# A fused attention read and ReLU-squared FFN on one core: the opening parts go from six to four, and GpSimd's steps of the weights and of batches 0 and 1 go to VectorE

## The chip, the core and the metric

The kernel runs on one core of a Trainium2 chip. The metric is the device time of one execution in microseconds (us), as the median of several runs. A core has TensorE (PE, with weight loads PEld), VectorE (DVE), ScalarE (ACT), GpSimd (POOL) and SyncE (SP), which here only issues DMAs. Each engine takes its instructions in order from a queue of its own.

## What is computed

Inputs are x (8 batches, 8 heads, 512 rows, 64 columns), a state (8, 8, 32, 64), and the weights w_in (512 x 2048) and w_out (2048 x 512), which come as float64.

```python
scores = scale * x @ state.T            # per batch and head: 512 x 32
a = softmax(scores);  xread = a @ state            # 512 x 64
a2 = softmax(scale * state @ x.T);  sread = a2 @ x # 32 x 64
x = concatenate([xread, sread])         # per batch 544 rows x 512
h = x @ w_in;  r = maximum(h, 0);  out = (r * r) @ w_out
```

## The kernel before, in words

**Precision.** Each product of float32 values is made of three matmuls of rounded parts: `split` (L96) writes hi, the rounded copy (ScalarE, L97), and lo, the rest (a subtraction, L98, on the engine that its last argument names). So a, z, g and the weights all have a hi and a lo tile.

**Weights.** w_in and w_out come as pairs of 32-bit words. `singles` (L100) makes float32 of 128 x 512 of them with one ScalarE instruction (L107) and four on VectorE: L108, L109 (one input each), L113, L117 (two inputs). There are 16 pieces of w_in (tiles w_raw, wf) and 16 of w_out (wo_raw, wof), that is 32 conversions. They share four buffers (tag "raw", RAW = 4), which L113 and L117 read last. The wo pieces are then split (L453), with wo_lo on GpSimd.

**z in place of w_in.** Since xread = a @ state, the kernel multiplies the state by w_in first (z_part, tile pz, L192 for the first six pieces and L204 later), stores z in device memory (zd) and reads it back for each batch and pair of column tiles (z_fetch, L230). Batches 0 to 3 use the first set of z, batches 4 to 7 a second set, which is made during batches 2 and 3.

**Attention.** For each batch two groups of four heads: scores (L291 or L301), a transposition (L306), the softmax over the state (soft1 and soft1b: maximum L317, subtraction L318, exponential L319 on ScalarE, sum L324, reciprocal L326, product L327), a transposition back (at, L329), and the split into a_hi and a_lo. L318 and L327 (tile q) are on GpSimd for batches 0 to 2 and on VectorE from batch 3; a_lo is on GpSimd for all.

**The FFN** (mlp, L383 on) goes in units: one column tile of 128 of w_in's 2048 columns (fc, 0 to 15) for one batch's 512 rows. `up` makes ph from a and z with six matmuls (L394), then r = relu (L396), the square (ScalarE L398 for the first ten units, VectorE L400 after that) and g_hi, g_lo. `down` makes twelve matmuls into four accumulators po (L420), two units behind.

**Order of the work.** Every batch needs all 16 pieces of both weights, which have to be loaded and converted first. So batches 0 and 1 are taken in parts, listed in BOTH: entry (b, c) means that batch b goes on up to column tile c. At the end of a part its four accumulators are copied to the tile `sum` (L439, L441) or added to it (L601). Steps of the weights and of the attention are spread over the units by due times (class Ahead): a weight's steps are due shortly before the first unit that needs its tile, the attention of a batch before that batch's first unit (2 x begins[b] - 1). From what is written out so, a scheduler sets the order on each engine, moving instructions ahead by its own estimate. SyncE's queue holds all loads and the stores of wf (wd, L165) and reads of zd (L230) in one order: a store that waits for VectorE, or a read that waits for an earlier store of zd, holds back the loads behind it.

Of the kernel before, what the change touches and what calls it, by code (L numbers as in the profile page):

```python
# [18 lines left out]
def memory_attention_then_relu2_ffn(  # L19
# [22 lines left out]
    nc = tc.nc  # L42
    P = 128
# [3 lines left out]
    N = stT.shape[1] // (H * B)  # L47
# [5 lines left out]
    NFC = DF // P  # L53
# [10 lines left out]
    XRAW = 2  # L64
    PLAIN_Z = 6
    PLAIN_X = 2
    BOTH = ((0, 2), (1, 6), (0, 10), (1, 10), (0, NFC), (1, NFC))
    LATE = 3

    def pool_early(early):  # L70
        return nc.gpsimd if early else nc.vector
# [11 lines left out]
    wo = [None] * NFCH  # L83
# [12 lines left out]
    def split(hi, lo, src, eng_lo):  # L96
        nc.scalar.copy(out=hi, in_=src)  # L97
        eng_lo.tensor_sub(out=lo, in0=src, in1=hi.bitcast(F32))  # L98

    def singles(out_f, words):  # L100

        low, high = words[..., 0], words[..., 1]
        bits = out_f.bitcast(I32)
        nc.scalar.activation(out_f, high.bitcast(F32), AF.Abs)  # L107
        nc.vector.tensor_scalar_max(out_f, out_f, 2.0**-15)  # L108
        nc.vector.tensor_scalar(  # L109
            out=bits, in0=bits, scalar1=3, scalar2=0x3FFFFFF8,  # L110
            op0=ALU.logical_shift_left, op1=ALU.bitwise_and,
        )
        nc.vector.scalar_tensor_tensor(  # L113
            out=bits, in0=high, scalar=-0x40000000, in1=bits,
            op0=ALU.bitwise_and, op1=ALU.bitwise_or,
        )
        nc.vector.scalar_tensor_tensor(  # L117
            out=bits, in0=low, scalar=29, in1=bits,
            op0=ALU.logical_shift_right, op1=ALU.bitwise_or,
        )  # L120
# [138 lines left out]
    def attention_group(b, g, pair):  # L259
        CG = C // NG  # L260
        NQ = CG // P
        NJ = S // 32
# [51 lines left out]
        def soft1():  # L314
            q1 = my["q1"]
            m1 = sb.tile([P, NJ, 1], F32, name="m1", bufs=2)
            nc.vector.tensor_reduce(out=m1[:, :, 0], in_=q1, axis=AX.X, op=ALU.max)  # L317
            pool_early(b < 3).tensor_sub(out=q1, in0=q1, in1=m1.broadcast_to([P, NJ, N]))  # L318
            nc.scalar.activation(q1, q1, AF.Exp)  # L319

        def soft1b():
            q1 = my["q1"]
            s1 = sb.tile([P, NJ, 1], F32, name="s1", bufs=2)
            nc.vector.tensor_reduce(out=s1[:, :, 0], in_=q1, axis=AX.X, op=ALU.add)  # L324
            nc.vector.tensor_scalar_add(s1, s1, EPS)
            nc.vector.reciprocal(s1, s1)  # L326
            pool_early(b < 3).tensor_mul(out=q1, in0=q1, in1=s1.broadcast_to([P, NJ, N]))  # L327
            at = sb.tile([P, S], F32, name="at", bufs=2)
            nc.vector.transpose(out=at, in_=q1.rearrange("p j n -> p (j n)"))  # L329
            split(pair[0][:, g, :], pair[1][:, g, :], at, nc.gpsimd)  # L330

        def cut_n():
            hl = sb.tile([P, NT, NQ, 2, P], F32R, name="xn_hl", tag="x_hl", bufs=1)
# [19 lines left out]
        def read():  # L353
# [16 lines left out]
            for q in range(NQ):  # L370
                for i in range(2):
# [5 lines left out]
                    )  # L377

        names = (load_t, cut_t, scores, soft1, soft1b, load_n, cut_n, turn, read)
        return {f.__name__: f for f in names}  # L380

# [61 lines left out]
    def wo_load(fc):  # L443
        k, i = divmod(fc, FPC)
        raw = sb.tile([P, DM, 2], I32, name="wo_raw", tag="raw", bufs=RAW)
        nc.sync.dma_start(
            out=raw.rearrange("p e w -> p (e w)"), in_=w_out[fc * P:(fc + 1) * P, :]
        )
        wf = sb.tile([P, DM], F32, name="wof", bufs=2)
        singles(wf, raw)  # L450
        if i == 0:
            wo[k] = [const.tile([P, FPC, DM], F32R, name=f"{n}{k}") for n in ("wo_hi", "wo_lo")]
        split(wo[k][0][:, i, :], wo[k][1][:, i, :], wf, nc.gpsimd)  # L453


    parts, upto = [], [0] * B
    for b, c in BOTH + tuple((b, NFC) for b in range(2, B)):
        parts.append((b, range(upto[b], c)))
        upto[b] = c

    begins, ends, at = {}, {}, {}
# [79 lines left out]
    for m in range(NFC):  # L541
        steps = []
        if m + 2 < NFC:
            steps.append(z0[m + 2][1])
        if m + 4 < NFC:
            steps.append(z0[m + 4][0])
        steps.append(lambda m=m: wo_load(m))
        if m >= 2:
            steps += z0[m][3]
        if m + 2 < NFC:  # L550
            steps.append(z0[m + 2][2])
        weights.add(steps, 2 * min(at[m], at[m - m % FPC] - 2))
# [62 lines left out]
    for i in range(NGB):  # L615
        pt = ps_x.tile([P, NCC, P], F32, name="pt2", tag="px")
        for cc in range(NCC):
            nc.tensor.transpose(
                out=pt[:, cc, :], in_=sr[i][:, cc * P:(cc + 1) * P], identity=ident
# [56 lines left out]
```

## Time and profile before

| | |
|---|---|
| median of 3 runs | 734.75 us (734.13 to 735.08) |
| profiled execution | 734.07 us, its span 732.2 us |
| TensorE busy | 679.1 us, 93% of the span |
| VectorE busy | 476.6 us, 65% |
| ScalarE busy | 392.7 us, 54% |
| GpSimd busy | 197.6 us, 27% |
| DMA | 90.52 MB, 124 GB/s over the span |
| granted TensorE clock, mean | 0.963 |

The page cuts the span into 40 slices of 18.3 us and gives each engine's busy share in tenths. In a row of a group stand: line, engine, operation, output<-input, shape, count | busy us, mean ns | idle us just before, and what ended it. In a row of the timeline stand: start and length in us, engine, line, operation, and in brackets the idle time before it with its releaser. Shares over the whole span hide that the opening and the rest have different limits, so the stages are read apart.

### The profile page before, as it was taken

The numbers are of one execution on the slowest core, as the hardware profiler recorded it, in microseconds if no ns is written. First come the engines' busy times: TensorE is split into PE (matmuls) and PEld (weight loads), VectorE is DVE, ScalarE is ACT, GpSimd is POOL, SyncE is SP. The second block draws the span as 40 slices with busy tenths as digits, with TensorE's granted clock in tenths as the row PEclk, the third lists the DMA queues.
The fourth block names the chain that finished last, engine by engine and source line by source line (L and its number), as shares of the span: only waits on it lengthen the run. The fifth ranks groups of instructions, "written<-read, shape, count | busy, mean of one in ns | idle before, by whom it ended". The sixth has DMA issues, their size and how long they took to land.

```text
span 732.2 us, 9312 instructions
## 1 busy us (share of the span) xinstructions
PE 679.1 (93%) x3152; PEld 554.3 (76%) x3152; DVE 476.6 (65%) x797; ACT 392.7 (54%) x711; POOL 197.6 (27%) x181
## 2 busy tenths in 40 slices
PE   4865898889999899999999999999999999999994
PEld 1434677768888788888888878878888888888893
DVE  5889798798956944356954694797755445443541
ACT  2656477566766664357654554656554345332441
POOL 2334121146662540025402322343152022000000
PEclk9677799999999999999999999999999999999998
DMA  9757877684464641143433211422141012100410
GB/s 265 252 175 249 243 244 235 201 221 133 133 213 129 195 127 59 47 140 119 136 108 116 86 59 58 143 87 86 60 144 58 31 33 82 42 1 9 135 59 30
DMA packets 72435, 90.52 MB, mean 124 GB/s; under 512 B 3780, under 2 KB 55748, under 8 KB 72388
## 3 DMA queue, kind: packets, MB, share of 16 engines
q1 hardware_dynamic: 54980, 73.15, 32.2%
q10 hardware_dynamic: 17408, 16.78, 6.8%
q8 instruction: 25, 0.41, 0.3%
q14 instruction: 22, 0.18, 0.1%
HBM read 60.03 MB, written 29.88 MB: 123 GB/s over the span
## 4 chain that ended last, share of the span: by engine, by line
PE 74%; DMA 11%; DVE 8%; ACT 3%; issue 2%; SPq 0%; POOL 0%; ACTq 0%; DVEq 0%
PE po L420 43%; PE ph L394 23%; DMA wo_raw<-w_out 3%; DMA z_raw<-zd 3%; PE pr L357 2%; PE pz L204 2%; DMA xn_raw<-xn 2%; DMA st_f<-stT 1%; PE pq L291 1%; DMA zd<-z_stage 1%; DVE sp_hl L252 1%; PE pz L192 1%; DVE wof L113 1%; DVE wof L117 1%; PE pt L345 1%
## 5 line engine op out<-in xcount | busy, mean ns | idle before, releaser
L420 PE MATMUL po<-wo_hi,g_hi 128*128 128x512 f32 x544 | 219.1, 405 | 15.5 <-ACT g_hi L97 12.1
L420 PE MATMUL po<-wo_lo,g_hi 128*128 128x512 f32 x544 | 216.4, 399 | 0.0
L400 DVE TENSOR_TENSOR ph<-ph,r 128x512 f32<-128x512 f32 (+1 forms) x134 | 89.0, 664 | 152.0 <-ACT r L396 151.9
L396 ACT ACTIVATE r<-ph 128x512 f32<-128x512 f32 (+1 forms) x144 | 82.6, 574 | 168.1 <-PE ph L394 167.4
L420 PE MATMUL po<-wo_hi,g_lo 128*128 128x512 f32 x544 | 152.4, 392 | 0.4
L420 PEld LDWEIGHTS po<-wo_hi,g_hi 128*128 128x128 f32 x544 | 103.9, 191 | 39.9 <-ACT g_hi L97 14.7
L420 PEld LDWEIGHTS po<-wo_lo,g_hi 128*128 128x128 f32 x544 | 104.9, 193 | 20.3 <-issue 0.7
L420 PEld LDWEIGHTS po<-wo_hi,g_lo 128*128 128x128 f32 x544 | 101.3, 189 | 22.0 <-DVE g_lo L98 1.6
L98 DVE TENSOR_TENSOR g_lo<-ph,g_hi 128x512 fp32r<-128x512 f32 (+1 forms) x144 | 94.5, 656 | 34.2 <-ACT g_hi L97 24.6
L97 ACT CAST g_hi<-ph 128x512 fp32r<-128x512 f32 (+1 forms) x144 | 81.1, 563 | 43.0 <-DVE ph L400 37.8
L394 PE MATMUL ph<-a_hi,z_hi 128*128 128x512 f32 x256 | 81.4, 399 | 0.6 <-DVE g_lo L98 0.6
L394 PE MATMUL ph<-a_hi,z_lo 128*128 128x512 f32 x256 | 79.7, 393 | 0.0
L394 PE MATMUL ph<-a_lo,z_hi 128*128 128x512 f32 x256 | 79.3, 391 | 0.0
L98 POOL TENSOR_TENSOR xn_hl<-xn_raw,xn_hl 128x1024 fp32r<-128x1024 f32 x16 | 39.2, 2449 | 147.9 <-ACT xn_hl L97 79.6
L183 POOL TENSOR_TENSOR w<-wf,w 64x512 fp32r<-64x512 f32 x32 | 43.5, 1360 | 59.6 <-ACT w L182 52.5
L394 PEld LDWEIGHTS ph<-a_hi,z_lo 128*128 128x128 f32 x256 | 48.4, 189 | 11.0 <-DVE z_lo L98 0.3
L394 PEld LDWEIGHTS ph<-a_hi,z_hi 128*128 128x128 f32 x256 | 47.8, 193 | 11.5 <-DVE g_lo L98 1.3
L394 PEld LDWEIGHTS ph<-a_lo,z_hi 128*128 128x128 f32 x256 | 48.2, 189 | 10.3
L98 DVE TENSOR_TENSOR z_lo<-z_raw,z_hi 128x512 fp32r<-128x512 f32 x64 | 50.2, 784 | 4.3 <-ACT z_hi L97 4.3
L97 ACT CAST z_hi<-z_raw 128x512 fp32r<-128x512 f32 x64 | 39.4, 615 | 12.3 <-DMA z_raw<-zd 11.9
L98 POOL TENSOR_TENSOR xt_hl<-xt_raw,xt_hl 128x1024 fp32r<-128x1024 f32 x12 | 29.3, 2438 | 58.5 <-ACT xt_hl L97 36.0
L98 POOL TENSOR_TENSOR wo_lo<-wof,wo_hi 128x512 fp32r<-128x512 f32 x16 | 22.5, 1407 | 79.4 <-ACT wo_hi L97 79.4
(98 smaller groups left out, 854.4 us busy)
## 6 DMA issues: line engine op xcount, KB each, us to landing
zd<-z_stage ACTq DMA_DIRECT2D x64, 256.0 KB
z_raw<-zd SPq DMA_DIRECT2D x63, 256.0 KB
xt_raw<-xT SPq DMA_DIRECT2D x16, 512.0 KB
w_raw<-w_in SPq DMA_DIRECT2D x16, 512.0 KB
wo_raw<-w_out SPq DMA_DIRECT2D x16, 512.0 KB
xn_raw<-xn SPq DMA_DIRECT2D x16, 512.0 KB
out<-sum SPq DMA_DIRECT2D x32, 256.0 KB
wd<-wf SPq DMA_DIRECT2D x16, 256.0 KB
```

Source lines behind the costliest of these rows:

```text
L97: nc.scalar.copy(out=hi, in_=src)
L98: eng_lo.tensor_sub(out=lo, in0=src, in1=hi.bitcast(F32))
L113: nc.vector.scalar_tensor_tensor(out=bits, in0=high, scalar=-0x40000000, in1=bits, op0=ALU.bitwise_and, op1=ALU.bitwise_or,)
L117: nc.vector.scalar_tensor_tensor(out=bits, in0=low, scalar=29, in1=bits, op0=ALU.logical_shift_right, op1=ALU.bitwise_or,)
L183: nc.gpsimd.tensor_sub(out=w[other], in0=wf[own], in1=w[own].bitcast(F32))
L192: nc.tensor.matmul(pz[:, q, :], lhsT=st["raw"][own, h, :], rhs=box["wf"][own, q, :], start=True, stop=True,)
L204: nc.tensor.matmul(pz[:, q, :], lhsT=a[:, h, :], rhs=w, start=j == 0, stop=j == len(todo) - 1,)
L357: nc.tensor.matmul(pr[:, q].rearrange("p i c -> p (i c)"), lhsT=my["e"][:, t, q].rearrange("p i n -> p (i n)"), rhs=my["xn"][:, t, q].rear ...
L394: nc.tensor.matmul(ph, lhsT=w, rhs=v, start=i == 0, stop=i == len(todo) - 1)
L396: nc.scalar.activation(r, ph, AF.Relu)
L400: nc.vector.tensor_mul(out=ph, in0=ph, in1=r)
L420: nc.tensor.matmul(po[t], lhsT=g, rhs=w, start=i == 0 and j == 0, stop=i == last and j == 2)
```

## The change

Batches 0 and 1 are taken in four parts instead of six: batch 0's tiles 0 to 5, batch 1's 0 to 9, batch 0's 6 to 15, batch 1's 10 to 15. Before: batch 0's 0 and 1, batch 1's 0 to 5, batch 0's 2 to 9, batch 1's 6 to 9, batch 0's 10 to 15, batch 1's 10 to 15. And three kinds of steps go from GpSimd to VectorE: L318 and L327 for batches 0 and 1 (8 instructions), a_lo for batches 0 and 1 (4), and wo_lo (16).

```diff
-    BOTH = ((0, 2), (1, 6), (0, 10), (1, 10), (0, NFC), (1, NFC))
+    BOTH = ((0, 6), (1, 10), (0, NFC), (1, NFC))
...
-            pool_early(b < 3).tensor_sub(out=q1, in0=q1, in1=m1.broadcast_to([P, NJ, N]))
+            pool_early(b == 2).tensor_sub(out=q1, in0=q1, in1=m1.broadcast_to([P, NJ, N]))
...
-            pool_early(b < 3).tensor_mul(out=q1, in0=q1, in1=s1.broadcast_to([P, NJ, N]))
+            pool_early(b == 2).tensor_mul(out=q1, in0=q1, in1=s1.broadcast_to([P, NJ, N]))
...
-            split(pair[0][:, g, :], pair[1][:, g, :], at, nc.gpsimd)
+            split(pair[0][:, g, :], pair[1][:, g, :], at, pool_early(b >= 2))
...
-        split(wo[k][0][:, i, :], wo[k][1][:, i, :], wf, nc.gpsimd)
+        split(wo[k][0][:, i, :], wo[k][1][:, i, :], wf, nc.vector)
```

Order on TensorE after the first two units, before; ph_456 and ph_513 are the up products of units 2 and 3, a_hi_289 is batch 1's attention:

```order
L394 MATMUL ph_456<-a_hi_289,z_hi_459 128x512
L394 MATMUL ph_456<-a_hi_289,z_lo_460 128x512 x2
L394 MATMUL ph_456<-a_lo_290,z_hi_459 128x512
L394 MATMUL ph_513<-a_hi_289,z_hi_459 128x512
L394 MATMUL ph_513<-a_hi_289,z_lo_460 128x512 x2
L394 MATMUL ph_513<-a_lo_290,z_hi_459 128x512
```

The same units on TensorE in the changed kernel; a_hi_109 is batch 0's attention, z_hi_401 its z of tiles 2 and 3, and pz_534 is z of tile 6:

```order
L394 MATMUL ph_398<-a_hi_109,z_hi_401 128x512 x2
L394 MATMUL ph_508<-a_hi_109,z_hi_401 128x512 x2
L204 MATMUL pz_534<-w2_0_430,stz_lo_125 128x256
L204 MATMUL pz_534<-w2_0_430,stz_hi_124 128x256
L394 MATMUL ph_398<-a_hi_109,z_lo_402 128x512 x2
L394 MATMUL ph_398<-a_lo_110,z_hi_401 128x512 x2
L394 MATMUL ph_508<-a_hi_109,z_lo_402 128x512 x2
L394 MATMUL ph_508<-a_lo_110,z_hi_401 128x512 x2
```

Units 2 and 3 are now batch 0's tiles 2 and 3, with new z, instead of batch 1's tiles 0 and 1.

Order on VectorE just ahead of the seventh g_lo (unit 6, g_lo_695), before; wof_609 and wof_700 are pieces 6 and 7 of w_out, counted from 0:

```order
L113 SCALAR_TENSOR_TENSOR wof_609<-wo_raw_607,wof_609 128x512
L117 SCALAR_TENSOR_TENSOR wf_758<-w_raw_589,wf_758 128x512
L117 SCALAR_TENSOR_TENSOR wof_609<-wo_raw_607,wof_609 128x512
L108 TENSOR_SCALAR wof_700<-wof_700 128x512
L109 TENSOR_SCALAR wof_700<-wof_700 128x512
L98 TENSOR_TENSOR w2_1_741<-wf_669,w2_0_740 128x512
L113 SCALAR_TENSOR_TENSOR wof_700<-wo_raw_698,wof_700 128x512
L98 TENSOR_TENSOR g_lo_695<-ph_678,g_hi_694 128x512
```

On VectorE in the changed kernel, a little ahead of the seventh g_lo; a_lo_311 is batch 1's attention, wo_lo2_393 and wo_lo3_531 belong to pieces 5 and 6 of w_out, po0_479 is batch 0's first accumulator:

```order
L98 TENSOR_TENSOR wo_lo2_393<-wof_445,wo_hi2_392 128x512
L329 STREAM_TRANSPOSE at_687<-q1_573 128x512
L109 TENSOR_SCALAR wf_811<-wf_811 128x512
L117 SCALAR_TENSOR_TENSOR wof_524<-wo_raw_522,wof_524 128x512
L98 TENSOR_TENSOR w2_1_794<-wf_703,w2_0_793 128x512
L108 TENSOR_SCALAR wof_632<-wof_632 128x512
L441 COPY sum_736<-po0_479 128x512
L113 SCALAR_TENSOR_TENSOR wf_811<-w_raw_607,wf_811 128x512
L98 TENSOR_TENSOR a_lo_311<-at_687,a_hi_310 128x512
L441 COPY sum_736<-po2_481 128x512
L98 TENSOR_TENSOR wo_lo3_531<-wof_524,wo_hi3_530 128x512
```

The moved steps stand between the conversions now, and the last a_lo of batch 1, which unit 6 needs, comes after the conversion of piece 6 of w_out. On GpSimd the first steps after its memsets are those of batch 2 (xt_hl).

## The prediction

> **What bounds the kernel now.** I read the page's slices first, then the busy times by stage, then what TensorE waits for, then VectorE's instruction groups up to 160 us, then single instructions.
>
> ```profile
> PE   4865898889999899999999999999999999999994
> DVE  5889798798956944356954694797755445443541
> PEclk9677799999999999999999999999999999999998
> ```
>
> TensorE is busy nine tenths and more from the ninth slice on. Only the first nine of forty (18.3 us each, to 165 us) and the last have room, and there VectorE is at 7 to 9 tenths.
>
> ```profile
> core 0: us, PE busy (x) PEld busy (x) DVE busy (x) ACT busy (x) POOL busy (x), PEclk, DMA share, GB/s
> 0.00:100.00 100.00, 68.87 (x222) 45.51 (x223) 79.12 (x142) 54.16 (x103) 30.55 (x32) 0.80 0.76 235
> 100.00:163.00 63.00, 55.14 (x264) 44.58 (x262) 54.73 (x86) 39.69 (x75) 15.54 (x12) 0.97 0.74 226
> 163.00:240.00 77.00, 76.82 (x360) 63.98 (x361) 58.72 (x102) 53.51 (x95) 41.51 (x34) 0.98 0.49 151
> 240.00:732.00 492.00, 478.24 (x2310) 400.26 (x2308) 284.05 (x471) 245.34 (x442) 110.01 (x106) 0.99 0.26 84
> ```
>
> TensorE idles 31.1 us before 100 us, 7.9 us from 100 to 163, 0.2 us from there to 240, and 13.8 us later, which the change does not touch. What the opening saves by the moment TensorE stops waiting (163.2 us) is saved at the end. What that moment waits for:
>
> ```profile
> 160.19 1.65 DVE L117 SCALAR_TENSOR_TENSOR wof<-wo_raw,wof 128x512 int32<-128x512 int32 x1
> ...
> 164.16 0.68 DVE L98 TENSOR_TENSOR g_lo<-ph,g_hi 128x512 fp32r<-128x512 f32 x1
> ```
> ```profile
> 99.51 0.40 PE L420 MATMUL po<-wo_hi,g_hi 128*128 128x512 f32 x1
> ...
> 163.18 0.77 PE L420 MATMUL po<-wo_hi,g_hi 128*128 128x512 f32 x1 [2.58 <-ACT g_hi L97]
> ```
>
> TensorE's last wait there (2.58 us, at 163.18) ends when ScalarE rounds the 17th unit's g, and in front of its square on VectorE (in-order) stands the last weight conversion; 164.16 is the 17th g_lo. I use "17th g_lo" as the mark. A unit is one column tile of one batch; 163.18 is the down product of number 16, counted from 0, and 99.51 that of number 6. So VectorE's queue up to that mark sets the opening, with the loads that it waits for.
>
> **The change, part by part.** First the price of a moved step. VectorE alone, and beside GpSimd:
>
> ```profile
> 72.44 0.68 DVE L113 SCALAR_TENSOR_TENSOR wof<-wo_raw,wof 128x512 int32<-128x512 int32 x1
> 73.05 0.68 DVE L117 SCALAR_TENSOR_TENSOR wf<-w_raw,wf 128x512 int32<-128x512 int32 x1
> ...
> 75.19 0.41 DVE L109 TENSOR_SCALAR wf<-wf 128x512 int32<-128x512 int32 x1
> ```
> ```profile
> 53.35 1.49 POOL L98 TENSOR_TENSOR a_lo<-at,a_hi 128x512 fp32r<-128x512 f32 x1 [4.36 <-ACT a_hi L97]
> 53.64 1.24 DVE L325 TENSOR_SCALAR s<-s 128x16 f32<-128x16 f32 x1
> 56.05 1.10 POOL L327 TENSOR_TENSOR q<-q,s 128x512 f32<-128x512 f32 x1 [1.21 <-DVE s L326]
> 56.17 1.53 DVE L113 SCALAR_TENSOR_TENSOR wf<-w_raw,wf 128x512 int32<-128x512 int32 x1
> ```
>
> Alone, a 128x512 step with two inputs lasts 0.68 us and the next starts 0.60 after it; one with one input lasts 0.41. Beside a GpSimd step the same L113 lasts 1.53, and a 16-column step 1.24. What this costs VectorE in the first 160 us (the last column is its idle time):
>
> ```profile
> L113 DVE SCALAR_TENSOR_TENSOR wf<-w_raw,wf 128x512 int32<-128x512 int32 x16 | 15.2, 949 | 0.1
> L113 DVE SCALAR_TENSOR_TENSOR wof<-wo_raw,wof 128x512 int32<-128x512 int32 x16 | 13.3, 834 | 0.1
> L117 DVE SCALAR_TENSOR_TENSOR wof<-wo_raw,wof 128x512 int32<-128x512 int32 x15 | 12.5, 831 | 0.1
> L117 DVE SCALAR_TENSOR_TENSOR wf<-w_raw,wf 128x512 int32<-128x512 int32 x16 | 11.9, 746 | 0.0
> L108 DVE TENSOR_SCALAR wof<-wof 128x512 f32<-128x512 f32 x16 | 9.0, 560 | 7.7 <-ACT wof L107 7.7
> L109 DVE TENSOR_SCALAR wof<-wof 128x512 int32<-128x512 int32 x16 | 8.6, 540 | 0.2
> L98 DVE TENSOR_TENSOR w<-wf,w 128x512 fp32r<-128x512 f32 x10 | 8.6, 859 | 0.2
> L108 DVE TENSOR_SCALAR wf<-wf 128x512 f32<-128x512 f32 x16 | 8.0, 500 | 9.4 <-ACT wf L107 9.4
> L98 DVE TENSOR_TENSOR z_lo<-z_raw,z_hi 128x512 fp32r<-128x512 f32 x10 | 7.9, 789 | 4.3 <-ACT z_hi L97 4.3
> L109 DVE TENSOR_SCALAR wf<-wf 128x512 int32<-128x512 int32 x16 | 7.7, 484 | 0.2
> ```
> ```profile
> L98 POOL TENSOR_TENSOR wo_lo<-wof,wo_hi 128x512 fp32r<-128x512 f32 x15 | 21.2, 1416 | 78.1 <-ACT wo_hi L97 78.1
> L98 POOL TENSOR_TENSOR a_lo<-at,a_hi 128x512 fp32r<-128x512 f32 x4 | 5.7, 1428 | 10.0 <-ACT a_hi L97 10.0
> L327 POOL TENSOR_TENSOR q<-q,s 128x512 f32<-128x512 f32 x4 | 4.7, 1176 | 7.9 <-DVE s L326 7.9
> L318 POOL TENSOR_TENSOR q<-q,m 128x512 f32<-128x512 f32 x4 | 4.6, 1139 | 18.0 <-DVE m L317 18.0
> L183 POOL TENSOR_TENSOR w<-wf,w 64x512 fp32r<-64x512 f32 x2 | 3.0, 1484 | 0.2
> L98 POOL TENSOR_TENSOR xt_hl<-xt_raw,xt_hl 128x1024 fp32r<-128x1024 f32 x1 | 2.8, 2777 | 0.6 <-ACT xt_hl L97 0.6
> ```
>
> Count times (mean less 0.68, or less 0.41 for L108 and L109), group by group: 4.3 + 2.5 + 2.3 + 1.1 + 2.4 + 2.1 + 1.8 + 1.4 + 1.1 + 1.2 = 20.2 us of stretch, beside 42.0 us of GpSimd steps (0.48 us each us). Of those 42.0 the change takes away the first four rows, 36.2, so 36.2 x 0.48 = 17.4 us of stretch goes, or all 20.2 if the others' share falls with them. I take 18.
>
> The Trainium skill, "SBUF — State Buffer", section "Who interferes with whom", says that the port pair shared by VectorE and GpSimd is an exclusive lock: whoever comes second is blocked until the first has finished. The rows agree that it blocks (1.24 us for a 16-column step). If every moved step blocked VectorE for its whole length, 36.2 us would come back instead of 18; that is the fourth rival.
>
> *Steps moved to VectorE.* 16 wo_lo, 8 q and 4 a_lo are 28 steps at 0.60 = +16.8 us. By the order of both kernels, VectorE's queue up to the 17th g_lo differs in little else: one sum copy and three sum additions fewer (-2.4), and seven steps of batch 2's attention earlier, six of about 0.6 (+3.6). Together +18.0. In all there are eight sum additions (L601) fewer; where they would fall, later, TensorE does not wait for VectorE, so the rest counts nothing.
>
> *Idle time of VectorE.* 17.1 us (9.4 + 7.7 in the L108 rows) is waiting for weight loads by way of ScalarE. A load's buffer is free when the fourth conversion before it is done. Conversions now stand 18.0 / 32 = 0.56 us further apart in VectorE's own work, so 2.2 us more of each load lies under work. Some 4.8 us of these waits are in the first 24 us, where nothing moves ahead of them; of the other 12.3 I take half, 6. Bounds: 0 (SyncE issues the loads in order, each still behind stores of wf that wait for VectorE) and 12.
>
> *Six tiles of batch 0 first.* Weights 2 to 5 are now due at units 2 to 5 instead of 4 to 7, batch 1's attention at unit 6 instead of 2. From unit 12 on both orders need each weight at the same unit, and both read z the same 63 times; what changes hands is the work ahead of unit 6. At the seventh g_lo (unit 6) VectorE's queue holds 19 moved steps (11.4) and 5.9 us of later weights more, +17.3. Before, it stood here:
>
> ```profile
> 100.02 0.68 DVE L98 TENSOR_TENSOR g_lo<-ph,g_hi 128x512 fp32r<-128x512 f32 x1
> ```
>
> Of GpSimd's 30.55 us to 100 us xt_hl's 2.8 and some 3.6 of memsets stay and 24 go, so 24 x 0.48 = 11.6 us of stretch; with 2 of the idle time, unit 6's g_lo comes at 100 + 17.3 - 11.6 - 2 = 104. That is 4 us late, with 5.9 us of weights done beforehand. What TensorE needs from there:
>
> ```profile
> 192.75 1.39 PE ph L394 x6
> 194.14 2.72 PE po L420 x12
> ```
> ```profile
> 110.18 0.28 PE L204 MATMUL pz<-w,stz_lo 128*128 128x256 f32 x1
> ...
> 111.38 0.40 PE L204 MATMUL pz<-w,stz_hi 128*128 128x256 f32 x2
> ```
>
> A unit is 1.39 + 2.72 = 4.1 us, a weight's twelve pz matmuls 1.4. Ten units and the last four weights are 46.7 us: from 104 to 151 without a wait, to 159 with all the 7.9 us of waits it has there now. So TensorE allows the mark at 151 to 159, against 164.
>
> *Sum* at the mark: +18.0 - 18 - 6 = -6 us, 164.2 to 158.2, inside what TensorE allows. The profiled execution took 734.07 us (span 732.2): 728.1. It is 0.7 under the median of 734.75, so 728.7. With the bounds (stretch 17.4 to 20.2, waits 0 to 12) the sum is +0.6 to -14.2; for the likely case alone 722 to 732.5.
>
> **The rivals.** *Slower: batch 1's attention comes too late.* Unit 6 waits for a_lo of batch 1, which now stands on VectorE behind the conversions of tiles 0 to 6; on SyncE two reads of zd stand in a row, and the weight loads behind them wait until those stores have landed. If unit 6's g_lo slips to 112, TensorE ends unit 16's wait at 112 + 46.7 + 7.9 - 0.5 = 166.1, and at 115 at 169.1, against 163.2: +3 to +6, say 738.7. It decides from 109. For it: the low clock (0.80) and 31 us of idle time up to 100 show how tight the chain is. Against: the estimate is 104. Chance 0.18.
>
> *Same: the loads set the pace.* The stretch pays for the moved steps, and VectorE's waits stay 17 us: 18 - 18 = 0, 734.7. For it: DMA engines are busy 0.74 to 0.76 of the time to 163. Against: at no time up to there at their limit for long. Chance 0.13.
>
> *Slower: VectorE pays in full.* If the stretch came from something else than GpSimd, +18: 752.7. Against: the rows at 53 and 56 us. Chance 0.04. The Trainium skill, "Perfetto Trace Analysis", section "Identifying the Most-Contended Engine", points this way: it picks the engine to relieve by occupancy, which would have VectorE relieved, not loaded.
>
> *Much faster: each moved step had blocked VectorE throughout.* 18 - 36.2 - 6 = -24, but TensorE cannot have the 17th unit before 99.5 + 46.7 = 146.2, so -17: 717.7. Against: 20.2 us of stretch is all that the groups show. Chance 0.05.
>
> **How the numbers follow.** The forecast has 0.60. Three runs lie within 0.13% of each other; 0.2% is about what a measurement can tell from no change, 1.5 us. Faster: 0.60 + 0.05 = 0.65; same 0.13; slower 0.18 + 0.04 = 0.22. From 720 to 738 the range leaves out the fourth rival (0.05), the third (0.04) and the later half of the first (0.09).
>
> **What would show it.** In the changed profile, L113 and L117 on VectorE should have means near 0.68 to 160 us and GpSimd almost nothing there; the seventh g_lo should stand at about 104 us, the 17th at about 158; TensorE's idle time from 100 to 163 should fall below 7.9 us. L113 means still above 0.80 would refute the stretch; a seventh g_lo after 109 would mean the first rival; L108 waits of 17 us still, with the rest as forecast, the second.

## The result and the profile after

The changed kernel took 727.07 us (723.7 to 730.17, 4 runs), the kernel before 734.44 us beside it (733.62 to 735.08): ratio 0.990, 95% interval 0.985 to 0.995. It is 7.4 us faster; 6 were forecast. The profiled execution took 723.7 us with a span of 721.9, the lowest of its four runs, so its trace flatters the change by about 3 us against the median.

Slices of the span after, as shown of before:

```profile
PE   4787679989999999999999999999999999999994
DVE  5979889998457853354975884897754436443551
```

The picture is the same: TensorE has room in the first nine slices, and VectorE stands at 7 to 9 tenths in eight of them. By stages (columns as before):

```profile
core 0: us, PE busy (x) PEld busy (x) DVE busy (x) ACT busy (x) POOL busy (x), PEclk, DMA share, GB/s
0.00:100.00 100.00, 68.45 (x244) 45.92 (x244) 82.63 (x171) 60.60 (x115) 6.26 (x13) 0.86 0.82 267
100.00:163.00 63.00, 58.32 (x266) 47.26 (x266) 58.23 (x102) 44.55 (x80) 14.59 (x8) 0.96 0.70 211
163.00:240.00 77.00, 76.99 (x370) 64.75 (x371) 50.64 (x86) 45.57 (x81) 30.19 (x27) 1.00 0.42 137
240.00:719.00 479.00, 469.43 (x2275) 393.67 (x2273) 277.58 (x462) 242.89 (x437) 109.53 (x106) 1.00 0.25 83
```

To 100 us GpSimd's busy time fell from 30.55 to 6.26 us, and VectorE does 171 instructions instead of 142 in 3.5 us more. TensorE's idle time from 100 to 163 fell from 7.9 to 4.7 us. The number in brackets behind PE is the better measure: 880 matmuls stand before 240 us (244 + 266 + 370), against 846 before. From 163 us on a matmul takes 77.0 / 370 = 0.21 us; 34 of them are 7.1 of the 10.4 us between the two profiled executions. In this pair and in the runs below the count gives the difference of the profiled times to within some 3 us, and I use it beside the 17th g_lo. It is rough: it takes a narrow matmul of z (256 columns) for as much as one of 512.

VectorE's groups to 160 us, and the two g_lo of the prediction:

```profile
L117 DVE SCALAR_TENSOR_TENSOR wof<-wo_raw,wof 128x512 int32<-128x512 int32 x16 | 12.5, 778 | 0.0
L113 DVE SCALAR_TENSOR_TENSOR wof<-wo_raw,wof 128x512 int32<-128x512 int32 x16 | 11.9, 742 | 0.0
L113 DVE SCALAR_TENSOR_TENSOR wf<-w_raw,wf 128x512 int32<-128x512 int32 x16 | 10.9, 683 | 0.1
...
L108 DVE TENSOR_SCALAR wof<-wof 128x512 f32<-128x512 f32 x16 | 7.2, 452 | 4.7 <-ACT wof L107 4.6
L108 DVE TENSOR_SCALAR wf<-wf 128x512 f32<-128x512 f32 x16 | 6.7, 420 | 5.7 <-ACT wf L107 5.6
```
```profile
101.13 0.68 DVE L98 TENSOR_TENSOR g_lo<-ph,g_hi 128x512 fp32r<-128x512 f32 x1
...
157.94 0.68 DVE L98 TENSOR_TENSOR g_lo<-ph,g_hi 128x512 fp32r<-128x512 f32 x1
```

L113 and L117 stand at 0.68 to 0.78 us (0.75 to 0.95 before), the waits of L108 at 10.4 us (17.1 before), the seventh g_lo at 101.1 and the 17th at 157.9. The signs that the prediction named came as named, but for one: GpSimd was to do almost nothing to 160 us and still does 13.5 us from 100 to 160, in steps that the change leaves on it. Whether the signs came for its reasons, the experiments decide, and for one of them they did not.

### The profile page after: what moved, and what is told of

It reads as the page before. It is cut to its first block, busy times and chain, and to the rows that moved or that the text cites. A ratio compares the mean times of both kernels' runs of the same rounds, so it can differ in the third digit from the quotient of the medians.

```text
span 721.9 us, 9304 instructions
## 1 busy us (share of the span) xinstructions
PE 673.2 (93%) x3152; PEld 551.6 (76%) x3152; DVE 469.1 (65%) x817; ACT 393.6 (55%) x711; POOL 160.6 (22%) x153
## 4 chain that ended last, share of the span: by engine, by line
PE 72%; DMA 11%; DVE 10%; ACT 3%; issue 2%; SPq 1%; ACTq 0%; DVEq 0%
PE po L420 43%; PE ph L394 23%; DMA wo_raw<-w_out 3%; DMA w_raw<-w_in 3%; PE pr L357 2%; PE pz L204 2%; DMA st_f<-stT 1%; DMA st_raw<-stT 1%; DVE sp_hl L252 1%; PE pq L291 1%; DMA z_raw<-zd 1%; PE pt L345 1%; DVE wo_lo L98 1%; DMA wd<-wf 1%; DVE z_lo L98 1%
## 5 line engine op out<-in xcount | busy, mean ns | idle before, releaser
L420 PE MATMUL po<-wo_hi,g_hi 128*128 128x512 f32 x544 | 215.1, 399 | 6.3 <-ACT wo_hi L97 2.9
L420 PE MATMUL po<-wo_lo,g_hi 128*128 128x512 f32 x544 | 213.0, 394 | 0.9 <-DVE wo_lo L98 0.9
L400 DVE TENSOR_TENSOR ph<-ph,r 128x512 f32<-128x512 f32 (+1 forms) x134 | 89.0, 665 | 162.7 <-ACT r L396 162.5
L420 PEld LDWEIGHTS po<-wo_lo,g_hi 128*128 128x128 f32 x544 | 103.2, 190 | 21.3 <-DVE wo_lo L98 1.3
L98 DVE TENSOR_TENSOR z_lo<-z_raw,z_hi 128x512 fp32r<-128x512 f32 x64 | 48.6, 759 | 3.3 <-ACT z_hi L97 3.3
L216 ACT COPY z_stage<-pz 128x512 f32<-128x512 f32 x64 | 37.1, 586 | 3.7 <-PE pz L204 2.5
```

The lines of the kernel that those rows point to most:

```text
L216: nc.scalar.copy(out=stage, in_=pz)
L400: nc.vector.tensor_mul(out=ph, in0=ph, in1=r)
L420: nc.tensor.matmul(po[t], lhsT=g, rhs=w, start=i == 0 and j == 0, stop=i == last and j == 2)
```

## The experiments

The theory at the start was the prediction's: the moved steps are paid by the stretch that goes away, and the gain comes from VectorE's waits for weight loads. The rivals: the gain comes from the order of the parts, or from neither alone.

**The order alone.** Only the list of the parts is changed; all steps stay on GpSimd.

```diff
-    BOTH = ((0, 2), (1, 6), (0, 10), (1, 10), (0, NFC), (1, NFC))
+    BOTH = ((0, 6), (1, 10), (0, NFC), (1, NFC))
```

> Only the opening parts go from six to four; all GpSimd steps stay. My theory (VectorE's queue up to the 17th g_lo sets the opening, and GpSimd steps stretch VectorE's): the stretch stays, so L113 of w_out's pieces keeps a mean near 0.83 us to 160 us, and the time moves by -1 us against before (from -4 to +3). Rival (the order makes the gain): -6 us or more.

726.10 us (725.47 to 726.99), ratio 0.991 (0.988 to 0.993): the whole gain of the change, as the rival said and not my theory. VectorE's groups to 160 us in this run:

```profile
L113 DVE SCALAR_TENSOR_TENSOR wf<-w_raw,wf 128x512 int32<-128x512 int32 x16 | 15.8, 989 | 0.0
...
L108 DVE TENSOR_SCALAR wf<-wf 128x512 f32<-128x512 f32 x16 | 9.3, 588 | 5.8 <-ACT wf L107 5.7
L108 DVE TENSOR_SCALAR wof<-wof 128x512 f32<-128x512 f32 x16 | 9.1, 570 | 5.0 <-ACT wof L107 5.0
```

The stretch is all there (L113 at 0.99 us, more than before), and still the waits of L108 are 10.8 us instead of 17.1. So the fall of the waits belongs to the order, not to the moved steps.

**The moved steps alone.** The order of before, the 28 steps on VectorE.

```diff
-            pool_early(b < 3).tensor_sub(out=q1, in0=q1, in1=m1.broadcast_to([P, NJ, N]))
+            pool_early(b == 2).tensor_sub(out=q1, in0=q1, in1=m1.broadcast_to([P, NJ, N]))
...
-        split(wo[k][0][:, i, :], wo[k][1][:, i, :], wf, nc.gpsimd)
+        split(wo[k][0][:, i, :], wo[k][1][:, i, :], wf, nc.vector)
```

> Only the 28 steps go to VectorE; six opening parts as before. My theory: 16.8 us of moved steps against 18 us of stretch and some 4 us of waits for loads: -4 us against before (from -2 to -8), L113 near 0.70 us. Rival (the order makes the gain, the engines nothing): within 1.5 us of before. Rival (VectorE pays in full): +10 or more.

748.45 us (746.5 to 750.15), ratio 1.021 (1.017 to 1.025): 15 us slower. By its time that is the last rival (+10 or more), but not by its way: the stretch is gone here as well (L113 of w_in's pieces at 0.68 us), and it is the waits of VectorE and TensorE that grow. Waits of VectorE to 165 us, and two of TensorE to 200 (in all us, times, longest):

```profile
DVE wf L108 <- ACT wf L107: 16.3, 8, 5.6
...
DVE wo_lo L98 <- ACT wo_hi L97: 5.4, 3, 3.9
```
```profile
PE ph L394 <- ACT a_hi L97: 8.1, 2, 7.8
PE ph L394 <- DVE g_lo L98: 6.1, 1, 6.1
```

TensorE waits 7.8 us for batch 1's attention, which this order needs at unit 2, but that is not where the time goes: by 160 us 467 matmuls stand here and 481 in the kernel before, 14 x 0.21 = 2.9 us. The 6.1 us end at 171.06 us, with the g_lo of unit 16. SyncE's queue, then ScalarE and VectorE, about that time:

```profile
150.86 0.50 SPq L446 DMA_DIRECT2D wo_raw<-w_out  x1
159.12 0.33 SPq L156 DMA_DIRECT2D wf<-wd  x1
...
161.08 1.26 SPq L131 DMA_DIRECT2D st_raw<-stT  x2
```
```profile
162.00 0.62 ACT L182 CAST w<-wf 64x512 fp32r<-64x512 f32 x1 [3.00 <-DMA wf<-wd]
164.19 1.71 DVE L98 TENSOR_TENSOR wo_lo<-wof,wo_hi 128x512 fp32r<-128x512 f32 x1 [3.91 <-ACT wo_hi L97]
...
168.32 0.59 ACT L97 CAST g_hi<-ph 128x512 fp32r<-128x512 f32 x1 [0.61 <-DVE ph L400]
173.80 1.04 ACT L97 CAST stz_hi<-st_raw 128x1024 fp32r<-128x1024 f32 x1 [4.90 <-DMA st_raw<-stT]
```

SyncE issues nothing between 150.86 and 159.12: it waits to read a weight back (L156) until its store, issued at 150.49 after a wait for VectorE's conversion, has landed. ScalarE waits 3.00 us for such a read, VectorE 3.91 us for ScalarE, and unit 16's g_lo comes at 170.32. The load of st_raw, issued behind those reads, lets ScalarE go on only at 173.80, after TensorE's 6.1 us; ScalarE, in order, stands still for 4.90 us, and TensorE waits 2.5 us more at 176.45. From 160 to 180 us 37 matmuls stand here, 73 in the kernel before, and from 180 to 200 us 81 against 105: 60 x 0.21 = 12.6 of the 16.0 us between the two profiled executions. A part of it is the granted clock, 0.50 from 170 to 180 us here and 1.00 in the kernel before.

**The change with wo_lo back on GpSimd, and with the attention's steps back there.**

```diff
-        split(wo[k][0][:, i, :], wo[k][1][:, i, :], wf, nc.vector)
+        split(wo[k][0][:, i, :], wo[k][1][:, i, :], wf, nc.gpsimd)
```

> The change, but wo_lo is on GpSimd again; the 12 steps of the attention stay on VectorE. My theory: 16 GpSimd steps of 1.4 us stretch VectorE by about 11 us and take 9.6 us of work from it: +1 to +4 us against the change, 728 to 731. Rival (order alone makes the gain): as the change, 727.

726.75 us (724.83 to 726.91), ratio 0.991 (0.987 to 0.994): the rival's figure, not the 728 to 731 of my theory.

```diff
-            split(pair[0][:, g, :], pair[1][:, g, :], at, pool_early(b >= 2))
+            split(pair[0][:, g, :], pair[1][:, g, :], at, nc.gpsimd)
```

(L318 and L327 go back likewise.)

> The change, but L318, L327 and a_lo of batches 0 and 1 are on GpSimd again; wo_lo stays on VectorE. My theory: 12 GpSimd steps stretch VectorE by about 7 us against 7.2 us of work taken from it: 0 to +3 us against the change, 727 to 730. Rival (batch 1's attention, late on VectorE, is what costs): 2 us or more faster than the change.

728.05 us (727.07 to 729.98), ratio 0.994 (0.991 to 0.996). With the new order, where these steps stand makes no difference that the intervals can tell.

**The change again**, beside the next three.

> The change once more, for its spread on one chip beside the two that follow: 724 to 730 us. No theory is told apart by it.

727.01 us (726.21 to 727.38), ratio 0.990 (0.986 to 0.993). Its profiled execution has the 17th g_lo at 161.70, 3.8 us after the first one's, and 865 matmuls before 240 us, 15 fewer (3.2 us); it took 3.65 us longer. One execution places the 17th g_lo to within some 4 us only.

**GpSimd busy again, by steps that read and by steps that only write.** After each wo_lo on VectorE a GpSimd step with two inputs, or two memsets.

```diff
         split(wo[k][0][:, i, :], wo[k][1][:, i, :], wf, nc.vector)
+        nc.gpsimd.tensor_sub(out=wf, in0=wf, in1=wo[k][0][:, i, :].bitcast(F32))
```

> The change, and after each wo_lo on VectorE one GpSimd subtraction more, over the piece of w_out that is no longer needed (wof): 16 steps of about 1.35 us that read SBUF; the output is not touched. My theory (GpSimd steps stretch VectorE's, 0.48 us for each us): about 10 us of stretch to the mark, L113 of w_out's pieces back above 0.80 us, +4 to +10 us against the change. Rival (the stretch came from elsewhere): within 1.5 us of the change, L113 below 0.75.

```diff
         split(wo[k][0][:, i, :], wo[k][1][:, i, :], wf, nc.vector)
+        nc.gpsimd.memset(wf, 0.0)
+        nc.gpsimd.memset(wf, 0.0)
```

> As the run before, but each extra GpSimd step is replaced by two memsets of wof, about 1.1 us together, which read nothing. If what stretches VectorE is that both read SBUF: within 1.5 us of the change, L113 of w_out's pieces below 0.78. If any GpSimd write does it: +4 us or more, L113 above 0.80. The wait for wof's buffer is the same in both runs, so a cost of that wait alone would show in both.

The reads: 737.09 us (735.75 to 739.28), ratio 1.005 (1.003 to 1.007), 10 us slower than the change. The memsets: 722.64 us (721.5 to 723.94), ratio 0.983 (0.979 to 0.987), 4 us faster than it. The groups to 160 us, with the reads first:

```profile
L113 DVE SCALAR_TENSOR_TENSOR wof<-wo_raw,wof 128x512 int32<-128x512 int32 x16 | 14.4, 901 | 0.1
...
L454 POOL TENSOR_TENSOR wof<-wof,wo_hi 128x512 f32<-128x512 f32 x15 | 29.5, 1968 | 97.9 <-DVE wo_lo L98 97.2 <-PE ph L394 0.7
```
```profile
L113 DVE SCALAR_TENSOR_TENSOR wof<-wo_raw,wof 128x512 int32<-128x512 int32 x16 | 11.4, 714 | 0.0
...
L455 POOL MEMSET wof<- 128x512 f32 x16 | 10.2, 641 | 0.7
L454 POOL MEMSET wof<- 128x512 f32 x16 | 9.4, 589 | 107.3 <-DVE wo_lo L98 107.3
```

Beside 29.5 us of reading steps L113 takes 0.90 us, beside 19.6 us of memsets 0.71. Both hold the wof buffer after wo_lo, the reads for 1.97 us and the memsets for 1.23, so a wait for it alone is not what costs; that the other 0.7 us of holding costs nothing was not tried. The stretch of L113 goes with GpSimd's reads. The Trainium skill, "SBUF — State Buffer", section "Who interferes with whom", says that a VectorE instruction with two SBUF inputs contends with a GpSimd instruction that reads SBUF and not with one that only writes it; these two runs agree. Why the memsets gain 4 us stays open: every edit also changes the order that the scheduler writes.

**The squares of units 10 to 17 on ScalarE, on top of the change.**

```diff
-            if units[0] < 10:
+            if units[0] < 18:
```

> The change, with the squares of units 10 to 17 on ScalarE instead of VectorE (18 instead of 10 units): 7 or 8 steps of 0.60 us less on VectorE up to the 17th g_lo, 4.5 us. My theory (VectorE's queue sets the mark): 2 to 4.5 us faster than the change. Rival (the weight loads set the pace): no change within 1.5 us. Rival (ScalarE, at 0.7 of the time from 100 to 160 us, becomes the bound): slower.

719.94 us (719.03 to 720.97), ratio 0.980 (0.977 to 0.984): 7 us faster than the change and the fastest kernel of all, by more than was expected.

At this point the order was known to be the gain, and its cause was still open. The next run takes the order apart: a first part of six tiles, but six parts.

```diff
-    BOTH = ((0, 2), (1, 6), (0, 10), (1, 10), (0, NFC), (1, NFC))
+    BOTH = ((0, 6), (1, 6), (0, 10), (1, 10), (0, NFC), (1, NFC))
```

> Only the first entry of the list of parts is changed, (0, 2) to (0, 6); there are still six parts, and all steps stay on the engines of before. First theory: the gain of the new order comes from the first part alone (batch 1's attention is needed at unit 6 instead of 2, so that the weights go ahead of it and their loads are issued earlier). Then this kernel gains what the order gained, -7 us: 725 to 729, about 500 matmul records by 163 us and 870 to 880 by 240, waits of L108 on VectorE of 11 us, not 17. Rival: the gain comes from the number of parts (two parts and eight additions to sum fewer, on VectorE). Then it stays within 2 us of before, 731.5 to 735.5, with 840 to 850 records by 240 us.

732.88 us (731.84 to 735.29), ratio 0.999 (0.997 to 1.001): no gain. The first theory falls, and the time stays where the rival put it. This run and the order alone differ in two ends of parts, after units 11 and 19 (units 5, 15, 25 and 31 end a part in both), and so in the batch to which units 12 to 19 belong. Their stages, six parts first:

```profile
0.00:140.00 140.00, 102.15 (x406) 75.48 (x406) 119.68 (x206) 83.74 (x158) 42.68 (x39) 0.87 0.82 257
140.00:180.00 40.00, 35.36 (x154) 26.73 (x155) 35.72 (x61) 28.76 (x51) 23.72 (x16) 1.00 0.48 142
180.00:240.00 60.00, 60.00 (x289) 50.45 (x288) 37.13 (x61) 36.11 (x63) 24.02 (x23) 1.00 0.39 127
```
```profile
0.00:140.00 140.00, 101.58 (x405) 75.49 (x406) 118.97 (x208) 84.57 (x160) 43.73 (x39) 0.87 0.81 258
140.00:180.00 40.00, 38.46 (x180) 31.54 (x179) 33.26 (x55) 28.28 (x51) 22.04 (x15) 1.00 0.47 140
180.00:240.00 60.00, 60.00 (x290) 50.48 (x289) 34.55 (x56) 34.45 (x62) 22.58 (x22) 1.00 0.39 130
```

To 140 us the two run alike (406 and 405 matmuls), from 180 on too. All of the difference lies between: 154 against 180 matmuls, 26 x 0.21 = 5.5 of the 6.8 us between the two medians. The end of a part after unit 19 has its additions at 183.72 us, where TensorE is busy throughout in both, so TensorE loses nothing by it. What is between, on TensorE, ScalarE and VectorE with six parts:

```profile
136.14 1.07 PE L420 MATMUL po<-wo_hi,g_lo 128*128 128x512 f32 x4
...
141.03 0.50 PE L420 MATMUL po<-wo_hi,g_hi 128*128 128x512 f32 x1 [1.03 <-ACT sum L439]
...
142.26 0.50 PE L420 MATMUL po<-wo_hi,g_hi 128*128 128x512 f32 x1 [0.49 <-DVE sum L441]
```
```profile
140.39 1.08 ACT L439 COPY sum<-po 128x512 f32<-128x512 f32 x2
```
```profile
139.18 0.69 DVE L400 TENSOR_TENSOR ph<-ph,r 128x512 f32<-128x512 f32 x1
...
140.23 1.38 DVE L109 TENSOR_SCALAR wof<-wof 128x512 int32<-128x512 int32 x1
141.53 0.68 DVE L441 COPY sum<-po 128x512 f32<-128x512 f32 x1
...
142.72 0.68 DVE L441 COPY sum<-po 128x512 f32<-128x512 f32 x1
143.32 0.68 DVE L98 TENSOR_TENSOR g_lo<-ph,g_hi 128x512 fp32r<-128x512 f32 x1
```

Up to unit 11 the two agree (its g_lo at 134.69, with four parts at 134.37); the square (L400) and the g_lo shown are unit 12's. With four parts they stand here, with the last conversion and the copies of that order behind them:

```profile
136.36 0.69 DVE L400 TENSOR_TENSOR ph<-ph,r 128x512 f32<-128x512 f32 x1
...
138.86 0.68 DVE L98 TENSOR_TENSOR g_lo<-ph,g_hi 128x512 fp32r<-128x512 f32 x1
...
147.56 0.69 DVE L117 SCALAR_TENSOR_TENSOR wof<-wo_raw,wof 128x512 int32<-128x512 int32 x1
...
156.89 1.28 DVE L441 COPY sum<-po 128x512 f32<-128x512 f32 x2
```

At the end of a part the next down product needs the four accumulators po, which must first be copied. Unit 11's last down products end at 137.2 us (136.14 + 1.07), but ScalarE's two copies begin at 140.39, behind the rounding of unit 12's g, and VectorE's stand in its in-order queue behind weight conversions and begin at 141.53 and 142.72. TensorE waits for the first (1.03 us, ScalarE's) and again for VectorE's (0.49), and unit 12's g_lo comes 4.5 us later, an offset that is still 5.0 us at the 17th g_lo (163.09 against 158.09). With four parts the part ends at 156 to 158 us, after the last conversion.

The copies are only a part of the loss, though. Of the 4.5 us, 2.8 are there before any of these copies begins: unit 12's square starts at 139.18 instead of 136.36, because its relu on ScalarE stands behind the rounding of a piece of w_out there (136.53 against 133.30). And from 160 to 180 us 85 matmuls stand against 96, where TensorE waits for no copy. Nor does the kernel before, whose time the six parts have, lose it so: up to 240 us no matmul of it waits for a copy or an addition, and two weight loads wait 0.7 us in all. It loses from 160 to 180 us, the kernel before first, then the order alone:

```profile
160.00:180.00 20.00, 17.42 (x73) 14.19 (x72) 16.66 (x30) 13.32 (x24) 12.75 (x8) 0.91 0.53 153
```
```profile
160.00:180.00 20.00, 20.00 (x96) 16.68 (x95) 19.15 (x36) 14.62 (x27) 10.48 (x7) 1.00 0.42 124
```

There stand TensorE's wait of 2.58 us at 163.18, and behind it matmuls of 0.63 us instead of 0.40 at a granted clock of 0.80 to 0.86 up to 170 us. The last conversion on VectorE starts at 160.19 in the kernel before and at 147.56 in the order alone. So the runs show that the list with two ends fewer takes 7 us less than either list with six parts, and where; by which way it does so is shown in part only, and differs between the two.

The waits of L108 in the run with six parts, to 160 us:

```profile
L108 DVE TENSOR_SCALAR wof<-wof 128x512 f32<-128x512 f32 x16 | 9.5, 594 | 5.1 <-ACT wof L107 5.1
L108 DVE TENSOR_SCALAR wf<-wf 128x512 f32<-128x512 f32 x16 | 9.3, 588 | 5.7 <-ACT wf L107 5.7
```

They are 10.8 us, as short as with the order alone, at the time of before: here shorter waits for loads did not make the kernel faster.

**wo_lo alone, and the attention's steps alone, in the order of before**, to find what makes the 28 steps cost 15 us there.

```diff
-        split(wo[k][0][:, i, :], wo[k][1][:, i, :], wf, nc.gpsimd)
+        split(wo[k][0][:, i, :], wo[k][1][:, i, :], wf, nc.vector)
```

> The parts of before; of the steps, only the 16 wo_lo go to VectorE. First theory: what made the moved steps dear in the old order (+15 us for all 28) is batch 1's attention, which that order needs at unit 2 and which then stood on VectorE behind other work. Then wo_lo alone costs little: 731 to 737, and the seventh g_lo stays at 98 to 103 us. Rival: each moved step costs alike, 16/28 of 15 = +8.6 us: 740 to 744.

733.32 us (729.88 to 736.61), ratio 1.000 (0.997 to 1.003).

```diff
-            split(pair[0][:, g, :], pair[1][:, g, :], at, nc.gpsimd)
+            split(pair[0][:, g, :], pair[1][:, g, :], at, pool_early(b >= 2))
```

(L318 and L327 of batches 0 and 1 go with it.)

> The parts of before; only L318, L327 and a_lo of batches 0 and 1 (12 steps) go to VectorE, wo_lo stays on GpSimd. First theory: this carries nearly all of the +15 us: 744 to 750, with a wait of TensorE of several us for a_hi or g_lo as with all 28 moved. Rival: each moved step costs alike, 12/28 of 15 = +6.4 us: 738 to 742. A third way: neither move alone costs, and only both together bring the queue late, under 737 here and in the run before.

733.09 us (725.75 to 734.52), ratio 0.999 (0.997 to 1.002). The third way that was named there: neither costs anything alone, only both together. Batch 1's attention alone is not the cause. In these two runs the load of st_raw is issued at 146.6 and 142.5 us, in the kernel before at 147.4, with both at 161.1. So the 15 us are not a price per step. That they come from one crossing of VectorE's queue and SyncE's, as the rows above suggest, is not shown: no run moves those reads and loads alone.

**The order and the squares without the moved steps.** The parts of the change, all steps as before, and units 10 to 17 squared on ScalarE.

> The new parts, all steps on the engines of before, and the squares of units 10 to 17 on ScalarE instead of VectorE (as in the run of the squares, which had the moved steps as well and took 719.9). First theory: what is left to gain is in VectorE's queue, whoever has the moved steps, which cost and return the same there: 718 to 722. Rival: that gain needs VectorE free of GpSimd's disturbance: 724 to 728, no better than the order alone (726.1).

726.64 us (726.41 to 727.7), ratio 0.991 (0.988 to 0.994). The rival holds: without the moved steps the squares gain nothing. From 140 to 160 us, in the change, with the squares on top, in the order alone, and in this run:

```profile
140.00:160.00 20.00, 16.29 (x66) 11.78 (x65) 19.80 (x29) 13.39 (x24) 10.47 (x5) 1.00 0.57 160
```
```profile
140.00:160.00 20.00, 19.24 (x86) 15.23 (x85) 15.87 (x27) 19.57 (x35) 11.86 (x7) 1.00 0.57 180
```
```profile
140.00:160.00 20.00, 18.46 (x86) 14.86 (x85) 14.11 (x20) 13.65 (x25) 11.55 (x8) 1.00 0.52 155
```
```profile
140.00:160.00 20.00, 18.95 (x90) 15.60 (x89) 11.42 (x14) 15.33 (x28) 10.08 (x8) 1.00 0.45 139
```

In the change VectorE is full there (19.80 of 20 us) and TensorE does 66 matmuls; the squares free 3.9 us of VectorE, and TensorE does 86. In the order alone VectorE has 5.9 us of room there, and taking squares off it adds four matmuls. So the moved steps do help up to 140 us (436 matmuls in the change and 423 in its second run, 405 with the order alone, by the same views) and give it back from 140 to 160, where VectorE's queue then ends late; that they gain with the squares is shown by the two times, the reading of why rests on these rows.

## Why the prediction was right, and where it was not

**Size and sign** were right (728.7 forecast, 727.07 measured), the reason was half right.

**The stretch pays for the moved steps (+18 - 18).** Right in the new order: with the steps on GpSimd 726.1 us, on VectorE 727.0, and L113 returns to 0.90 us when GpSimd is given reads. In VectorE's own queue the two terms were not equal: counted as in the forecast, the stretch fell from 20.2 to 5.1 us, 15 of the 18, and wo_lo took 0.85 us there instead of 0.68, so that the 28 steps, less the 0.08 us by which each overlaps the next, took 19.4 us and not 16.8. The bound was not a general one: in the old order the same exchange cost 15 us, through waits that the sum had no term for. There the mechanism that I had put down as the first rival (batch 1's attention late) shows as 7.8 us of TensorE's waiting, but only 2.9 us are lost by 160 us there, and with the attention's steps moved alone nothing is.

**Idle time of VectorE (-6).** This step failed. I wrote that conversions further apart would hide 2.2 us more of each load. The waits fell by 6.7 us, as forecast, but in the order alone by 6.3 with nothing moved, and with six parts just as much (5.7 and 5.1 us of waits) at the time of before. In that run shorter waits were worth nothing by themselves; that the term had nearly the size of the gain (6 against 7.4) is luck.

**Six tiles of batch 0 first, and the eight sum additions (priced at nothing).** This step failed too, and here is the gain. The size of the first part was indeed worth nothing (732.9 against 733.0), but the list with two ends of parts fewer is worth 7 us (726.1). I counted the copies and additions as VectorE's time (2.4 us up to the mark, nothing later). That later TensorE does not wait for VectorE holds: from 180 to 240 us it is busy throughout. What I did not ask is what an end of a part does while conversions still fill VectorE's queue: with six parts the next part's down products wait for copies, and the next unit's relu and square come later. That is seen against the run with six parts; how the same list shortens the kernel before, which waits for no copy, stays open.

**The marks.** Seventh g_lo 101.1 (104 forecast), 17th 157.9 (158.2). The second run of the change (103.7 and 161.7) shows how much of such agreement is chance, and in the run of the moved steps alone the mark is 6.2 us late (170.3 against 164.2) where the execution is 16.0 us longer, since TensorE waits behind the mark as well. The count of matmuls by a fixed time holds there: 776 by 240 us against 846, 70 x 0.21 = 14.7 us.

**The rivals.** Batch 1's attention was not too late in the new order (the seventh g_lo at 101.1, 109 was the limit), and the loads did not set the pace (10.4 us of waits, not 17). VectorE paying in full (+18) did not come in the new order. The rule of occupancy behind it, in the Trainium skill's "Perfetto Trace Analysis", section "Identifying the Most-Contended Engine", is right about the next step: taking eight squares off the full engine gave the 7 us of the fastest kernel. In the order alone, where VectorE was busy 14.11 of the same 20 us, it gave nothing. Much faster (-17) did not come either.

## What to carry to other kernels

When work is split into parts that share accumulators, count the ends of the parts, ask what stands in the queue ahead of the copies that free them, and try the list of parts by itself. Price an exchange between two engines in the order in which it will run: the same 28 steps cost nothing in one order and 15 us in another, and neither half of them cost anything alone. A sum that meets the measured time is not shown by that; here one term that the runs gave no worth of its own and one that was left out had nearly the same size.

## What the runs showed of the hardware

- A GpSimd subtraction of 128x512 with two inputs took 1.97 us on average beside VectorE's conversions, and VectorE's L113 then 0.90 us instead of 0.74; memsets of the same size took 0.59 and 0.64 on average and left it at 0.71.
- The first down matmul after a wait is longer than those behind it: 0.50 us against 0.40 at 141.03 and 142.26 us, and the next starts 0.34 and 0.33 us after it instead of 0.23, so a wait costs TensorE 0.1 us more than its idle time shows.
- After the wait of 6.06 us in the run of the moved steps alone the granted clock read 0.50 from 170 to 180 us, and matmuls took 0.63 us instead of 0.40; after the waits of about 1 us at 141.03 (six parts) and 146.04 us (order alone) it stayed at 1.00.
- Three runs of before lay within 0.13%; 25 runs beside the last experiments spread from 730.11 to 736.7 us, and one run of the attention alone took 725.75. Differences under 2 us were not told apart here.
